# First expert's weights: one rounding instruction on ScalarE, remainders on VectorE instead of GpSimd

## The chip, the cores and the metric

The kernel runs on one core of a Trainium2 chip. A core has five engines with a queue of instructions each: TensorE (PE, with its weight loads PEld), VectorE (DVE), ScalarE (ACT), GpSimd (POOL) and SyncE (SP), which here issues most DMA transfers. The metric is the device time of one execution in microseconds, lower is better.

## What is computed

Attention with random features over 64 heads (8 batches of 8), then a mixture of experts in which each of 4608 tokens goes to one of eight experts.

```python
# attention, per batch and head; m = 128 features, D = 64
h = x_scaled @ omega.T - sum(x_scaled * x_scaled) / 2
phi = exp(h - max(h)) / sqrt(m)                 # for q and for k
kv = k_phi.T @ v;  z = sum(k_phi)
attn = (q_phi @ kv) / (q_phi @ z + 1e-6)
# experts, on x = attn as 4608 rows of 512
e = argmax(x @ w_gate);  gate = softmax(x @ w_gate)[e]
eom = sigmoid(x @ w_output_gate)
out = gate * eom[e] * (relu(x @ w1[e]) @ w2[e])  # w1: 512x1024, w2: 1024x512
```

## The kernel before

The 64 heads are taken in pairs of batches as 32 units of 1152 tokens (nine chunks of 128). The first eight units, u = 0 to 7, are handled in f32 by TensorE: a projection `pp` of three groups (L629, with GpSimd's squares L601 as one input), minima by VectorE (`mx`, L651) and biases (`nb`, L657), exponentials on ScalarE (`ex`, L670, tile `ef`), a sum over keys (`kv`, L766), a transposition of the queries (`tq`, L720), which ScalarE rounds to f16 (`th`, L725) and VectorE completes with the remainder (`tl`, L727), a product with the key sums (`pn`, L849) and a division on VectorE (`xf`, L858, L860, L862). GpSimd then splits the result into an f16 half and a remainder (`xs`, L880 and L884) and adds up gate logits (`lga`, L902). PSUM has eight banks; each of `pp`, `tq`, `kv` and `pn` takes one and holds it until the step that last reads it has run: `tl` for a `tq`, `ex` for a `pp`, the gate step `gl` (L816) for a `kv`, `xf` for a `pn`.

From unit 8 on the projection works with f16 halves and remainders. The first eight units make the first quarter of the tokens; then VectorE routes them (which expert, which place), writes a list, and GpSimd gathers the rows of the first items. An item is 128 tokens of one expert: two products with w1 and w2, each matrix kept as an f16 half (`w1h`, `w2h`) and an f16 remainder (`w1l`, `w2l`) so that three f16 products stand for one in f32.

The weights of the expert that is taken first (`FIRST = 1`) are loaded during the attention of the first units, in eight quarters of 128 x 1024: four of w1 and four of w2. SyncE loads a quarter into `r1` or `r2`; ScalarE multiplies it in place by 64 (step `w0s`, `scale_up`, L484); ScalarE rounds it to f16 (`w0h`, `rounded`, L488); GpSimd subtracts (`w0l`, `remainder`, L492). Weights of later experts are treated otherwise: `high` (L462) scales and rounds in one activation, `low` (L468) makes the remainder from the raw weights in one scalar_tensor_tensor on VectorE.

Nothing is scheduled at run time: a step is added to a plan with `plan.add` (its key, engine, what it comes after), and the table `ORDER` lists the steps by number in the order in which they are emitted. So each engine's queue is that table, cut to the engine. `BANKS` gives each step that needs a bank its number. An engine runs its queue in order and waits at an instruction until what it depends on is done.

Of the kernel before, what the change touches and what calls it, by code (L numbers as in the profile page):

```python
# [14 lines left out]
AF = mybir.ActivationFunctionType  # L15
# [312 lines left out]
def attention_moe(ctx: ExitStack, tc: tile.TileContext, kqt, kqn, v, om, wg, w1, w2, cf, cm, ci, out):  # L328
# [146 lines left out]
    def first_weights():  # L475
# [6 lines left out]
        def scale_up(which, i):  # L482
            src, _, _, sc = quarter(which, i)
            nc.scalar.activation(src, src, AF.Copy, scale=sc)  # L484

        def rounded(which, i):
            src, hi, _, _ = quarter(which, i)
            nc.scalar.copy(hi, src)  # L488
# [1385 lines left out]
```

## Time and profile before

| | us |
|---|---|
| median of three runs | 619.28 (617.71 to 622.87) |
| profiled execution, its time | 620.54 |
| profiled execution, its span | 618.5 |
| TensorE busy | 594.8 (96%) |
| TensorE weight loads | 471.3 (76%) |
| VectorE busy | 386.0 (62%) |
| ScalarE busy | 420.6 (68%) |
| GpSimd busy | 376.2 (61%) |

The shares are averages over the span. The stretches differ: the first eight units run to about 77 us, then come the units from 8 on together with the first routing, and from about 110 us the first items of the experts run beside the rest of the attention. Times in the rows below count from the start of the span.

### The profile page before, as it was taken

The page shows a single profiled execution, that of the slowest core. Times are in us where ns is not written, and L with a number is a line of the kernel's source. Part 1 is how long each engine was busy: PE and PEld are TensorE (multiplying, and loading weights), DVE is VectorE, ACT ScalarE, POOL GpSimd, SP SyncE. Part 2 cuts the span into 40 slices and gives each one's busy share as a digit, 9 for nine tenths or more (in the row PEclk, how much of TensorE's full clock was granted, in tenths as well). Part 3 has the DMA queues.
Part 4 walks back from the last instruction along what each step waited for, and adds up shares of the span by engine and source line. Part 5 has one row for each costly group of instructions (what it writes and reads, how often), then busy time and mean ns, then how long its engine had stood idle before and what let it go on. Part 6 is the DMA issues. An engine that isn't in the chain of part 4 may idle for free. (4 is left out here: it accounts for less than half of the span.)

```text
span 618.5 us, 22153 instructions
## 1 busy us (share of the span) xinstructions
PE 594.8 (96%) x8736; PEld 471.3 (76%) x8736; DVE 386.0 (62%) x1220; ACT 420.6 (68%) x978; POOL 376.2 (61%) x275
## 2 busy tenths in 40 slices
PE   8999987999999999999999999999999999999995
PEld 8999876877796777778777777778867587777775
DVE  4877699876678887657797856543693351162143
ACT  6999999779888688889958787872431341351244
POOL 2265689788977879997897889985322122121203
PEclk9999997899999999999999999999999899999999
DMA  8655688999999999989978999777586935942391
GB/s 282 196 158 159 212 274 212 233 236 257 305 251 217 254 281 242 269 188 238 304 199 251 247 192 203 171 170 222 193 176 189 245 82 109 300 117 69 104 278 50
DMA packets 146022, 128.86 MB, mean 208 GB/s; under 512 B 104286, under 2 KB 127584, under 8 KB 144608
## 3 DMA queue, kind: packets, MB, share of 16 engines
q1 hardware_dynamic: 139904, 107.45, 68.6%
q0 software_dynamic: 5984, 19.72, 10.1%
q8 instruction: 73, 1.20, 0.8%
q14 instruction: 61, 0.50, 0.3%
HBM read 83.86 MB, written 19.30 MB: 167 GB/s over the span
## 5 line engine op out<-in xcount | busy, mean ns | idle before, releaser
L1661 PE MATMUL ph<-xt,w1h 128*128 128x128 f16 (+1 forms) x2368 | 200.4, 218 | 2.2 <-ACT ef L670 0.7
L1661 PE MATMUL ph<-xt,w1l 128*128 128x128 f16 (+1 forms) x1184 | 196.6, 218 | 0.9 <-issue 0.9
L1661 PEld LDWEIGHTS <-w1h 128*128 128x128 f16 x2368 | 178.2, 98 | 9.6 <-issue 2.4
L670 ACT ACTIVATE ef<-pp,nb 128x128 f32<-128x128 f32 x576 | 163.7, 397 | 15.7 <-DVE nb L664 11.4
L651 DVE TENSOR_REDUCE pp<-pp 128x3 f32<-128x384 f32 x192 | 103.0, 557 | 35.2 <-PE pp L629 29.0
L693 POOL TENSOR_TENSOR es<-ef,es 128x1152 f16<-128x1152 f32 x44 | 104.8, 2390 | 25.8 <-ACT es L691 15.2
L1661 PEld LDWEIGHTS <-w1l 128*128 128x128 f16 x1184 | 115.2, 98 | 1.6 <-issue 1.6
L1672 DVE SCALAR_TENSOR_TENSOR hl<-ph,hh 128x512 f16<-128x512 f32 (+1 forms) x76 | 50.4, 664 | 95.2 <-ACTq L1555 53.5
L1693 PE MATMUL po<-w2h,hh 128*128 128x512 f16 x280 | 106.9, 382 | 0.4 <-ACT es L691 0.4
L1693 PE MATMUL po<-w2l,hh 128*128 128x512 f16 x280 | 106.8, 382 | 0.0
L1693 PE MATMUL po<-w2h,hl 128*128 128x512 f16 x280 | 106.7, 381 | 0.0
L1668 ACT ACTIVATE hh<-ph 128x512 f16<-128x512 f32 (+1 forms) x76 | 44.5, 591 | 85.5 <-PE ph L1661 65.7
L1693 PEld LDWEIGHTS <-hh 128*128 128x128 f16 x560 | 51.5, 98 | 53.7 <-issue 1.9
L1617 POOL DMA_INDIRECT gx<-rows,gi x38 | 39.5, 1038 | 83.3 <-ACT os L1772 34.4
L551 POOL TENSOR_TENSOR xlo<-xt,xhi 128x1152 f16<-128x1152 f32 x24 | 57.3, 2386 | 9.8 <-ACT xhi L544 8.0
L691 ACT CAST es<-ef 128x1152 f16<-128x1152 f32 x44 | 51.5, 1180 | 3.0 <-DMA et<-es 2.3
L1693 PEld LDWEIGHTS <-hl 128*128 128x128 f16 x280 | 27.5, 98 | 33.8 <-issue 0.8
L1772 ACT ACTIVATE os<-po,gx 128x512 f32<-128x512 f32 (+1 forms) x34 | 23.3, 686 | 43.5 <-PE po L1693 39.7
L849 PE MATMUL pn<-kvs,et 128*128 128x81 f16 (+1 forms) x960 | 47.9, 204 | 2.2 <-DVE nb L664 0.7
L849 PEld LDWEIGHTS <-et 128*128 128x128 f16 (+1 forms) x960 | 40.5, 101 | 9.3 <-issue 1.8
L629 PE MATMUL pp<-omh,xhi 64*128 64x128 f16 x432 | 42.9, 223 | 2.3 <-ACT ef L670 0.9
L1759 POOL DMA_INDIRECT out<-os,oi x25 | 26.6, 1065 | 27.7 <-ACT os L1772 22.9
(215 smaller groups left out, 1093.6 us busy)
## 6 DMA issues: line engine op xcount, KB each, us to landing
r<-w SPq DMA_DIRECT2D x10, 2048.0 KB
xt<-kqt SPq DMA_DIRECT2D x31, 576.0 KB
xn<-kqn SPq DMA_DIRECT2D x24, 576.0 KB
rawv<-v SPq DMA_DIRECT2D x32, 325.0 KB
rows<-xs SPq DMA_DIRECT2D x16, 576.0 KB
r<-w SPq DMA_DIRECT2D x8, 512.0 KB
ef<-w SPq DMA_DIRECT2D x2, 512.0 KB
et<-w SPq DMA_DIRECT2D x2, 512.0 KB
```

The costliest lines, as they stand in the source:

```text
L551: lambda t0=t0, t1=t1: nc.gpsimd.tensor_tensor(out=xl(u)[:, t0:t1], in0=xt32(u)[:, t0:t1], in1=xh(u)[:, t0:t1], op=ALU.subtract),
L629: nc.tensor.matmul(banks["pp", 2 * u + i, g][:, c, :], x[r, t], w[r, :], start=(a == 0), stop=(a == len(ops) - 1))
L651: nc.vector.tensor_reduce(out=pp[:, 3, 0:3], in_=pp[:, 0:3, :], op=ALU.min, axis=AX.X)
L670: nc.scalar.activation(ef(n)[:, c, :], banks["pp", n, g][:, c % 3, :], AF.Exp, bias=nb(n)[:, c : c + 1], scale=-SK)
L691: nc.scalar.copy(es(slot_es(n))[:, 0], ef(n))
L693: nc.gpsimd.tensor_tensor(out=es(slot_es(n))[:, 1], in0=ef(n), in1=es(slot_es(n))[:, 0], op=ALU.subtract)
L849: nc.tensor.matmul(pn[lo:hi, c - c0, :], a[:, c, lo:hi], w[:, :, b], start=(i == 0), stop=(i == len(ops) - 1))
L1617: nc.gpsimd.indirect_dma_start(out=gx(n), out_offset=None, in_=rows[0 : (j + 1) * NC * P], in_offset=bass.IndirectOffsetOnAxis(ap=tabs[gr] ...
L1661: nc.tensor.matmul(ph[:, f4, 0:w_], w[qd][:, kk, fo : fo + P], xt(n)[:, x, 0:w_], start=(a == 0), stop=(a == 3 * KC - 1))
L1668: nc.scalar.activation(hh(n)[:, sl, 0:w_], banks["ph", n, g][:, :, 0:w_], AF.Relu)
L1672: nc.vector.scalar_tensor_tensor(out=hl(n)[:, sl, 0:w_], in0=banks["ph", n, g][:, :, 0:w_], scalar=0.0, in1=hh(n)[:, sl, 0:w_], op0=ALU.ma ...
L1693: nc.tensor.matmul(po, x(n)[:, f, :], w[f // 2][:, f % 2, :], start=(f == 0 and a == 0), stop=(f == FC - 1 and a == 2))
```

## The change

The two ScalarE steps of a quarter, `w0s` and `w0h`, become one step `w0h` that calls `high`, the function of the later experts. The step `w0l` calls `low` on VectorE instead of `remainder` on GpSimd. The plan has 3310 steps instead of 3318, and all others stand in the same order; `BANKS` is unchanged.

```diff
-        def scale_up(which, i):
-            src, _, _, sc = quarter(which, i)
-            nc.scalar.activation(src, src, AF.Copy, scale=sc)
-
-        def rounded(which, i):
-            src, hi, _, _ = quarter(which, i)
-            nc.scalar.copy(hi, src)
-
-        def remainder(which, i):
-            src, hi, lo, _ = quarter(which, i)
-            nc.gpsimd.tensor_tensor(out=lo, in0=src, in1=hi, op=ALU.subtract)
-
...
                 plan.add(
-                    ("w0s", *key), ("ACT",), 0.95, lambda which=which, i=i: scale_up(which, i), after=[("w0", *key)], rank=R
+                    ("w0h", *key), ("ACT",), 0.95, lambda which=which, i=i: high(which, i), after=[("w0", *key)], rank=R
                 )
                 plan.add(
-                    ("w0h", *key), ("ACT",), 0.95, lambda which=which, i=i: rounded(which, i), after=[("w0s", *key)], rank=R
-                )
-                plan.add(
-                    ("w0l", *key), ("POOL",), 2.1, lambda which=which, i=i: remainder(which, i), after=[("w0h", *key)], rank=R
+                    ("w0l", *key), ("DVE",), 1.22, lambda which=which, i=i: low(which, i), after=[("w0h", *key)], rank=R
                 )
```

The functions that are now called for the first expert, too:

```python
def high(which, i, aside=False, n=None):
    src, hi, lo, sc = quarter(which, i, aside)
    ...
    nc.scalar.activation(hi, src, AF.Copy, scale=sc)

def low(which, i, aside=False, n=None):
    src, hi, lo, sc = quarter(which, i, aside)
    ...
    nc.vector.scalar_tensor_tensor(out=lo, in0=src, scalar=sc, in1=hi, op0=ALU.mult, op1=ALU.subtract)
```

The table `ORDER` is rewritten, since every number shifts; what it does is seen in the queues. From L492 on the line numbers of the changed kernel are 15 lower than before: L727 becomes L712, L651 L636, L657 L642, L816 L801, L788 L773, L862 L847.

VectorE's queue early in unit 0, before: the gate weights, the three `tl` steps of unit 0 (`et` from `tq`), then a minimum.

```order
L394 TENSOR_SCALAR wgs<-wgr 128x256
L395 SCALAR_TENSOR_TENSOR wgs<-wgr,wgs 128x256
L727 TENSOR_TENSOR et_283<-tq_1_260,et_283 128x384
L727 TENSOR_TENSOR et_283<-tq_0_250,et_283 128x384
L727 TENSOR_TENSOR et_283<-tq_2_269,et_283 128x384
L651 TENSOR_REDUCE pp_2_306<-pp_2_306 128x3
```

The same place of the changed kernel:

```order
L394 TENSOR_SCALAR wgs<-wgr 128x256
L395 SCALAR_TENSOR_TENSOR wgs<-wgr,wgs 128x256
L468 SCALAR_TENSOR_TENSOR w1l_95<-r_107,w1h_91 128x1024
L712 TENSOR_TENSOR et_283<-tq_1_260,et_283 128x384
L712 TENSOR_TENSOR et_283<-tq_0_250,et_283 128x384
L712 TENSOR_TENSOR et_283<-tq_2_269,et_283 128x384
L636 TENSOR_REDUCE pp_2_306<-pp_2_306 128x3
```

The remainder of w1's first quarter has come between the gate weights and the three `tl` steps.

VectorE's queue in unit 3, before: minima and biases, `tl` for groups 2 and 0 of unit 3 with unit 2's gate step between, and the key sums (`kvs`) of unit 3.

```order
L651 TENSOR_REDUCE pp_0_660<-pp_0_660 128x3
L651 TENSOR_REDUCE pp_1_691<-pp_1_691 128x3
L651 TENSOR_REDUCE pp_1_690<-pp_1_690 128x3
L657 TENSOR_SCALAR nb_718<-pp_1_690 128x3
L657 TENSOR_SCALAR nb_720<-pp_1_691 128x3
L727 TENSOR_TENSOR et_754<-tq_2_722,et_754 128x384
L816 SCALAR_TENSOR_TENSOR kvs_614<-kv_582,kvs_614 128x2x16
L727 TENSOR_TENSOR et_754<-tq_0_729,et_754 128x384
L788 SCALAR_TENSOR_TENSOR kvs_762<-kv_733,kvs_762 128x2x65
```

The same place of the changed kernel:

```order
L636 TENSOR_REDUCE pp_0_660<-pp_0_660 128x3
L468 SCALAR_TENSOR_TENSOR w2l_106<-r_108,w2h_102 128x1024
L636 TENSOR_REDUCE pp_1_691<-pp_1_691 128x3
L636 TENSOR_REDUCE pp_1_690<-pp_1_690 128x3
L642 TENSOR_SCALAR nb_719<-pp_1_690 128x3
L642 TENSOR_SCALAR nb_721<-pp_1_691 128x3
L712 TENSOR_TENSOR et_754<-tq_2_723,et_754 128x384
L801 SCALAR_TENSOR_TENSOR kvs_613<-kv_582,kvs_613 128x2x16
L468 SCALAR_TENSOR_TENSOR w1l_97<-r_107,w1h_93 128x1024
L712 TENSOR_TENSOR et_754<-tq_0_730,et_754 128x384
L773 SCALAR_TENSOR_TENSOR kvs_762<-kv_734,kvs_762 128x2x65
```

Two remainders are new here: w2's last quarter ahead of two minima, w1's third quarter between unit 2's gate step and the `tl` step that frees a bank of `tq`.

GpSimd's queue at its last remainders and the first gather, before (`es` and `xlo` are remainders of the attention, `gx` the gathered rows, `gi` the list that VectorE writes):

```order
L693 TENSOR_TENSOR es_1840<-ef_1775,es_1840 128x1152
L492 TENSOR_TENSOR w2l_104<-r_108,w2h_100 128x1024
L551 TENSOR_TENSOR xlo_1865<-xt_1755,xhi_1842 128x1152
L492 TENSOR_TENSOR w1l_96<-r_107,w1h_92 128x1024
L1555 UNCONDITIONAL_BRANCH x2
L1617 DMA gx_2315<-rows,gi_2092 128x528
```

The same place of the changed kernel:

```order
L678 TENSOR_TENSOR es_1836<-ef_1771,es_1836 128x1152
L536 TENSOR_TENSOR xlo_1858<-xt_1751,xhi_1838 128x1152
L1540 UNCONDITIONAL_BRANCH x2
L1602 DMA gx_2307<-rows,gi_2084 128x528
```

The two remainders are gone from GpSimd's queue ahead of the gather, and nothing has taken their place.

## Rows read from the trace of the kernel before

**Rows 1.** Table of stretches: bounds, length, busy time per engine, TensorE's granted clock, DMA.
```profile
core 0: us, PE busy (x) PEld busy (x) DVE busy (x) ACT busy (x) POOL busy (x), PEclk, DMA share, GB/s
8.00:73.00 65.00, 64.99 (x918) 60.83 (x916) 48.41 (x158) 61.35 (x184) 32.06 (x24) 1.00 0.62 197
77.00:110.00 33.00, 26.28 (x391) 23.07 (x391) 31.57 (x136) 30.45 (x89) 29.46 (x19) 0.84 0.84 233
125.00:480.00 355.00, 349.32 (x5458) 269.49 (x5456) 244.04 (x809) 263.98 (x599) 273.76 (x196) 1.00 0.92 229
```
**Rows 2.** TensorE's groups, 8 to 73 us: busy us, mean ns, idle time ahead.
```profile
L629 PE MATMUL pp<-omf,xt 64*128 64x128 f32 x260 | 27.8, 283 | 0.0
...
L810 PE MATMUL kv<-wgs,kvf 128*128 128x32 f16 x18 | 1.4, 177 | 0.0
```
**Rows 3.** Instructions on tile w1h: count, ns least/median/most, first and last start.
```profile
L462 ACT ACTIVATE w1h<-r x16: 1040/1047/1057, 174.3 to 547.4; 128x1024 f16<-128x1024 f32 x16
L468 DVE SCALAR_TENSOR_TENSOR w1l<-r,w1h x16: 1212/1218/1749, 175.6 to 548.6; 128x1024 f16<-128x1024 f32 x16
L488 ACT CAST w1h<-r x4: 1037/1072/1142, 23.3 to 64.6; 128x1024 f16<-128x1024 f32 x4
L492 POOL TENSOR_TENSOR w1l<-r,w1h x4: 2126/2134/2137, 68.9 to 107.1; 128x1024 f16<-128x1024 f32 x4
```
**Rows 4.** VectorE's timeline near 188 us: start, us, operation, count, idle before.
```profile
187.87 4.49 DVE L468 SCALAR_TENSOR_TENSOR w2l<-r,w2h 128x1024 f16<-128x1024 f32 x3 [1.24 <-ACT w2h L462]
```
**Rows 5.** GpSimd's timeline near 188 us.
```profile
187.55 1.44 POOL L714 TENSOR_TENSOR vs<-rawv,vs 128x650 f16<-128x650 f32 x1
```
**Rows 6.** VectorE's timeline near 102 us.
```profile
101.94 1.35 DVE L1065 TENSOR_TENSOR place<-cmt,rt 128x1152 f16<-128x1152 f16 x1
```
**Rows 7.** GpSimd's timeline near 102 us.
```profile
100.34 2.38 POOL L693 TENSOR_TENSOR es<-ef,es 128x1152 f16<-128x1152 f32 x1
```
**Rows 8.** Timelines of VectorE, GpSimd and TensorE, 14 to 19 us.
```profile
15.31 1.37 DVE L394 TENSOR_SCALAR wgs<-wgr 128x256 f16<-128x256 f32 x1
16.71 0.43 DVE L395 SCALAR_TENSOR_TENSOR wgs<-wgr,wgs 128x256 f16<-128x256 f32 x1
17.41 1.49 DVE L727 TENSOR_TENSOR et<-tq,et 128x384 f16<-128x384 f32 x3 [0.28 <-ACT et L725]
...
14.42 2.11 POOL L601 TENSOR_TENSOR xn<-xt 128x1152 f32<-128x1152 f32 x1 [4.27 <-DMA xt<-kqt]
...
18.51 0.36 PE L629 MATMUL pp<-half,xn 64*128 64x128 f32 x1
```
**Rows 9.** Timelines of VectorE and TensorE, 36 to 39 us.
```profile
36.55 0.57 DVE L651 TENSOR_REDUCE pp<-pp 128x3 f32<-128x384 f32 x1 [0.36 <-PE pp L629]
...
37.49 0.17 DVE L858 TENSOR_SCALAR den<-pn 128x5 f32<-128x5 f32 x1 [0.17 <-PE pn L849]
...
38.23 0.56 DVE L862 TENSOR_TENSOR xf<-pn,den 128x400 f32<-128x400 f32 x1
...
38.80 0.27 PE L629 MATMUL pp<-omf,xt 64*128 64x128 f32 x1
```
**Rows 10.** Timelines of VectorE, GpSimd, ScalarE and TensorE, 41 to 45 us.
```profile
42.40 0.55 DVE L727 TENSOR_TENSOR et<-tq,et 128x384 f16<-128x384 f32 x1
...
42.18 2.11 POOL L601 TENSOR_TENSOR xn<-xt 128x1152 f32<-128x1152 f32 x1 [0.60 <-DMA xt<-kqt]
...
41.91 1.08 ACT L484 ACTIVATE r<-r 128x1024 f32<-128x1024 f32 x1
...
44.77 0.49 PE L629 MATMUL pp<-omf,xt 64*128 64x128 f32 x4
```
**Rows 11.** Timelines of VectorE and TensorE, 48 to 50 us.
```profile
48.05 0.55 DVE L727 TENSOR_TENSOR et<-tq,et 128x384 f16<-128x384 f32 x1
...
49.23 0.95 PE L766 MATMUL kv<-rawv,ef 128*128 128x130 f32 x7
```
**Rows 12.** Timelines of VectorE and TensorE, 63 to 65 us.
```profile
63.58 0.55 DVE L727 TENSOR_TENSOR et<-tq,et 128x384 f16<-128x384 f32 x1
...
64.63 0.49 PE L629 MATMUL pp<-omf,xt 64*128 64x128 f32 x4
```

270 rows, old and new, of the table ORDER are left out of this document.

## The prediction

> **What bounds the kernel now.** I read the table of stretches first [rows 1]. From 8 to 73 us, where all eight quarters of the first expert's weights arrive and their rounding is done, TensorE is busy 64.99 of 65 us at full granted clock, ScalarE 61.35, VectorE 48.41, GpSimd 32.06. The list of TensorE's groups in that stretch [rows 2] says the same in another way: none of its seven groups (the first and the last are shown) had any idle time ahead of it. So TensorE bounds 8–73 us, and ScalarE, though 94% busy, is never waited for. From 77 to 110 us the order turns over: VectorE is busy 31.57 of 33 us, TensorE 26.28 and its granted clock is 0.84. This is the second attention stage together with the first routing, and VectorE bounds it. From 125 to 480 us TensorE is busy 349.32 of 355 us. Whatever delays TensorE before 73 us therefore has nowhere to be made up: it shifts the start of the VectorE stretch, and that shifts what comes after.
>
> **What is removed.** ScalarE loses eight rounding instructions of about 1.08 us (L488 in [rows 3]), 8.6 us in all; the scaling instruction becomes the rounding one (the same form exists as L462, 1.05 us) at the same place. Price: nothing, in either direction, because the stretch where ScalarE gets lighter is TensorE's (0.0 of waits in [rows 2]). GpSimd loses eight subtractions of 2.13 us (L492 in [rows 3]), 17.0 us. The last one starts at 107.1 us [rows 3], late in the stretch that VectorE bounds, and what follows it on GpSimd is the first gather, which needs a list that VectorE makes. Price: nothing again.
>
> **What is added.** VectorE gets eight subtractions of the form L468, 1.22 us each [rows 3]. Consecutive VectorE instructions overlap a little: three L727 take 1.49 us together [rows 8] and one takes 0.55 [rows 10], a pitch of 0.47, so 0.08 is hidden and each insertion costs its successors 1.14 us. That is 9.1 us of VectorE work in a stretch where VectorE is idle 16.6 of 65 us. So most of it could be absorbed; the question is at which of the eight places the next VectorE instruction gives TensorE a PSUM bank that it needs at once. I walked through them in program order.
>
> - First quarter of w1, straight behind the gate weights (L394, L395). L395 ends at 17.14 and the three L727 begin at 17.41, having waited for ScalarE [rows 8]. With the new instruction they begin at 17.06 + 1.14 = 18.20, later by 0.79. The second of them ended at 17.41 + 0.47 + 0.55 = 18.43 and gives back the bank in which TensorE's group at 18.51 starts [rows 8]. Slack there is almost nothing: TensorE **+0.77**.
> - First quarter of w2 and last quarter of w2 stand ahead of a reduction (L651) that waits for TensorE, and the third quarter of w2 ahead of an L727 that waits for ScalarE's casts. These holes hide them: **0**. Without the cover each would cost up to 1.14.
> - Second quarter of w1, ahead of the reduction at 36.55, which had waited 0.36 for TensorE. The new instruction starts behind the previous one at about 36.11 and ends 0.70 after the reduction could begin. The later idle of 0.17 and small gaps leave 0.43 at the division L862, which ends at 38.79; TensorE's group at 38.80 writes into the bank that it frees [rows 9]: **+0.43**.
> - Third quarter of w1, ahead of the L727 at 42.40. Its rounded half comes from ScalarE: the instruction at 41.91 ends at 42.99 [rows 10], with the 1.20 already lost 44.19. If it starts then, L727 ends about 45.9 and TensorE's group at 44.77 [rows 10], now due at 45.97, is just met: 0. But GpSimd's squares (L601, 2.11 us, before at 42.18) are pushed to about 43.95 by the work ahead of them (the neighbouring quarter's subtraction delays GpSimd's small sums). If VectorE must let them finish, it starts at 46.06, L727 runs 47.20–47.75, and TensorE waits from 45.97: **+1.8**.
> - Fourth quarter of w1, straight ahead of the L727 at 48.05, which ended at 48.60. With 1.14 more it ends at 49.74, against TensorE's group at 49.23 [rows 11], with some wake-up time: **+0.6**.
> - Second quarter of w2, straight ahead of the L727 at 63.58, end 64.13; with 1.14 more 65.27, against TensorE's group at 64.63 [rows 12]: **+0.65**.
>
> Must VectorE let GpSimd finish? In the trace a subtraction L468 that met GpSimd's L714 took longer: three of them cover 4.49 us where three pitches and an overlap would be 3.5, and GpSimd's L714 ran 187.55 to 188.99 across the first [rows 4, 5]. L394 of 256 columns took 1.37 us beside L601 (14.42 to 16.53) and ended just behind it, where L395, of the same 256 columns and with nothing beside it, took 0.43 [rows 8]. Against it: the 1152-column L1065 (1.35 us) ran inside GpSimd's L693 and was not stretched [rows 6, 7]. The first two are the nearest in form (an f32 source and L468 itself), so I take the +1.8, with the 0 as the other bound.
>
> The Trainium skill has a rule for this ("SBUF — State Buffer", section "SBUF: two separate sides"): a VectorE operation with two SBUF inputs and a GpSimd operation share a port pair that is an exclusive lock, and whichever starts first holds it for its whole instruction. The 4.49 us agree with it, the L1065 does not obviously. By the rule the third quarter of w1 costs the 1.8, without it 0: the sum would be 4.25 or 2.45.
>
> **Sum.** 0.77 + 0.43 + 1.8 + 0.6 + 0.65 = 4.25 us. The profiled execution took 620.54 us, so it would take 624.8; it was 1.26 above the median of three runs, 619.28, and on that median the forecast is **623.5 us**. A measurement of this kernel can tell about 1% (6.2 us) from no change, so this would be a change within 1%.
>
> **Rivals.** (a) No lock at the third quarter: 2.45, so 621.7 us. For it: the difference in start is only 0.2 us, and L1065. (b) All eight fit into VectorE's idle 16.6 us: 619.3 us. Against it: five places where the slack read from the rows is under 0.5 us. (c) TensorE's new waits lower its clock. In 77–110, where TensorE is idle a fifth of the time, the granted clock, a mean over its two levels of 1.2 and 2.4 GHz, is 0.84 against 1.00 [rows 1]; that is 0.16 × 33 = 5.3 us of lost clock for waits of about 2 us each. The 1.8 us wait is as long, so about half of that on top: 4.25 + 2.6 = 6.9, 626 us, up to 628 with more waits. (d) The other side: the kernel gets faster. If ScalarE's 8 × 0.95 = 7.6 us of relief (the pitch of its rounding) came through, the time would be 611.7 us. It decides from the point where TensorE waits for ScalarE in 8–73; the 0.0 of [rows 2] speak against it.
>
> **How the numbers follow.** Forecast (lock, +4.25) 0.36; (a) 0.27; (b) 0.12; (c) 0.19; (d) 0.06. The range of 617.5 to 628.0 us takes in the forecast, (a), (b) and (c), with some 1.5 us of scatter on either side as the three runs show, and leaves out (d) and what exceeds (c): about 0.14. Faster by over 1% (below 613.1) is (d), 0.06; slower by over 1% (above 625.5) is (c) and the upper edge of the forecast, 0.22; the rest is 0.72.
>
> **What would show it.** In the profile after: TensorE's waits of 0.4 to 1.8 us on VectorE's L727 and L862 (in their new line numbers) at about 18.5, 39, 46, 50 and 66 us; ScalarE lighter by 8 to 9 us and GpSimd by 17, VectorE heavier by 10; L468 at about 46 us ending behind GpSimd's squares; the stretch behind 77 us as long as before, only shifted. Wrong would be the forecast if TensorE still shows no waits in 8–73 (b), if its granted clock falls below 1.00 there (c), or if the stretch after 77 us is shorter, which nothing here predicts.

## The result, and the profile after

The changed kernel takes 625.79 us as the median of 22 runs (620.4 to 631.58), the kernel before, timed beside it, 620.54 (617.47 to 624.25). The ratio is 1.0069 with a 95% interval of 1.0047 to 1.0092: 4.3 us slower (2.9 to 5.7); the ratio leaves out the two longest runs of the changed kernel, which count as a slower state. A later comparison has the same (e12 below, 1.0062). The forecast was 4.25 us slower, a change within 1%. Its 623.5 us stood on a median of 619.28 us for the kernel before, which is 620.54 here: of the 2.3 us by which it missed the time, 1.3 lie there.

The profiled execution took 628.51 us, above that median; its span is 626.7 us. So the two profiles differ by 8 us where the medians differ by 5, and a part of what the traces show must be scatter between executions. The table of stretches of the changed kernel, with the columns of [rows 1]:

```profile
8.00:73.00 65.00, 62.58 (x856) 57.92 (x854) 53.87 (x155) 52.15 (x166) 27.29 (x20) 1.00 0.58 180
77.00:110.00 33.00, 23.55 (x387) 20.17 (x385) 29.68 (x124) 30.03 (x84) 22.05 (x16) 0.99 0.89 243
110.00:125.00 15.00, 13.06 (x190) 11.45 (x190) 12.15 (x56) 12.23 (x38) 7.54 (x5) 0.73 0.86 228
125.00:480.00 355.00, 349.68 (x5453) 270.66 (x5452) 248.80 (x824) 267.13 (x604) 274.39 (x195) 1.00 0.93 228
```

From 8 to 73 us TensorE is no longer full: 62.58 us of 65 against 64.99 in [rows 1], and 856 matmul records against 918. ScalarE and GpSimd became lighter there, VectorE heavier. From 125 us on the picture is the same as before.

TensorE's waits from 17 to 83 us, in the changed kernel (engine, line, released by; total us, times, longest):

```profile
PE pp L614 <- DVE et L712: 1.6, 2, 1.4
PE kv L751 <- DVE et L712: 0.6, 1, 0.6
PE pp L614 <- DVE xf L847: 0.3, 1, 0.3
PE pp L614 <- DVE nb L642: 0.2, 1, 0.2
```

In the kernel before nothing waited up to 73 us [rows 2]. The third line is not new: it stands at 80.0 us, and the kernel before has the same wait at 75.3 us:

```profile
PE pp L629 <- DVE xf L862: 0.3, 1, 0.3
```

All new waits are for VectorE, none for ScalarE or GpSimd. What the view lists as a wait is shorter than the delay that goes with it (0.20 us are listed at 69.37 us, where TensorE loses 0.68), so the table further down goes by the starts of the instructions.

The longest of them is the one at the third quarter of w1. VectorE's, GpSimd's and TensorE's timelines of the changed kernel there (start, us, operation, idle before):

```profile
44.73 2.70 DVE L468 SCALAR_TENSOR_TENSOR w1l<-r,w1h 128x1024 f16<-128x1024 f32 x1 [0.53 <-ACT w1h L462]
47.36 0.54 DVE L712 TENSOR_TENSOR et<-tq,et 128x384 f16<-128x384 f32 x1
...
44.25 2.10 POOL L586 TENSOR_TENSOR xn<-xt 128x1152 f32<-128x1152 f32 x1
...
47.96 0.49 PE L614 MATMUL pp<-omf,xt 64*128 64x128 f32 x4 [1.40 <-DVE et L712]
```

GpSimd's squares began 0.48 us before the remainder and ended at 46.35; the remainder ended 1.08 us later, as if it had begun only then. L712 came behind it, and TensorE waited 1.40 us for the bank. In [rows 10] the same step, there L727, stood in the queue without the remainder.

**Where the shift arises.** The n-th TensorE instruction is the same one in all these kernels, so its start in one trace less its start in the trace of before gives the shift of TensorE. The table has the growth of that shift over each place (the times are those of the trace of before), worked out for five kernels. The first two rows lie ahead of any remainder and have nothing to do with the places; what the first one is, the last section tells.

| place | forecast | changed | e12 (changed again) | e4 | e3 | e1 |
|---|---|---|---|---|---|---|
| up to 14 us (start) | 0 | 1.06 | 0.73 | 0.42 | 0.42 | 0.59 |
| 14–18.2, ahead of the first place | 0 | −0.14 | −0.14 | −0.62 | −0.62 | −0.21 |
| 18.2–18.8, w1 first quarter | 0.77 | 0.19 | 0.33 | 0.72 | 0.25 | 0.00 |
| 29.3–32.2, w2 first quarter | 0 | 0.13 | 0.12 | 0.13 | 0.13 | −0.01 |
| 38.1–39.4, w1 second quarter | 0.43 | 0.47 | 0.47 | 0.46 | 0.00 | 0.00 |
| 43.7–46.4, w1 third quarter | 1.8 | 1.47 | 1.47 | 0.00 | 0.00 | 0.00 |
| 46.4–50.8, w1 fourth quarter | 0.6 | 0.87 | 0.87 | 0.86 | 0.00 | 0.00 |
| 64.5–67.8, w2 second quarter | 0.65 | 0.68 | 0.68 | 0.68 | 0.00 | 0.00 |
| sum of the quarters | 4.25 | 3.81 | 3.94 | 2.85 | 0.38 | −0.01 |

From 83 us on it is scatter: the shift of the changed kernel's profiled execution is 4.74 us at 83 us and 8.34 at the end, that of e12, the same program, 4.54 and −3.34.

### The profile page after: what moved, and what is told of

Same layout as the page of the kernel before. It is cut to its first block, busy times and chain, and to the rows that moved or that the text cites. A ratio compares the mean times of both kernels' runs of the same rounds, so it can differ in the third digit from the quotient of the medians.

```text
span 626.7 us, 22148 instructions
## 1 busy us (share of the span) xinstructions
PE 596.2 (95%) x8736; PEld 473.0 (75%) x8736; DVE 395.9 (63%) x1228; ACT 416.1 (66%) x970; POOL 362.1 (58%) x267
## 5 line engine op out<-in xcount | busy, mean ns | idle before, releaser
L636 DVE TENSOR_REDUCE pp<-pp 128x3 f32<-128x384 f32 x192 | 102.9, 557 | 36.3 <-PE pp L614 31.2
L1757 ACT ACTIVATE os<-po,gx 128x512 f32<-128x512 f32 (+1 forms) x34 | 23.4, 687 | 43.2 <-PE po L1678 39.4
```

Source lines behind the costliest of these rows:

```text
L636: nc.vector.tensor_reduce(out=pp[:, 3, 0:3], in_=pp[:, 0:3, :], op=ALU.min, axis=AX.X)
```

## The experiments

**What is the price of VectorE's remainders alone?** In e1 they are left out, with the rest of the change kept.

```diff
+        for i in range(NQ):
+            nc.vector.memset(w1l[i], 0.0)
+            nc.gpsimd.memset(w2l[i], 0.0)
...
-                    ("w0l", *key), ("DVE",), 1.22, lambda which=which, i=i: low(which, i), after=[("w0h", *key)], rank=R
+                    ("w0l", *key), ("DVE",), 1.22, lambda which=which, i=i: None, after=[("w0h", *key)], rank=R
```

> The changed kernel with the eight VectorE remainders of the first expert left out (the f16 remainders are zeros, written once at the start), so it has the lighter ScalarE and the lighter GpSimd and nothing on VectorE. Theory (VectorE's insertions alone cost, the relief of ScalarE and GpSimd is worth nothing because TensorE never waits for them in 8-73 us): the time of the kernel before, within 1 us, and no wait of TensorE on L712-type steps. Rival (the relief is worth something that the insertions eat up again): faster than before by 2 to 7.6 us.

Measured: ratio 1.0003 (0.9969 to 1.0036). TensorE's only wait from 17 to 83 us, and the stretch 8–73 in the columns of [rows 1]:

```profile
PE pp L617 <- DVE xf L850: 0.3, 1, 0.3
...
8.00:73.00 65.00, 65.00 (x913) 61.04 (x912) 47.80 (x157) 55.34 (x177) 25.44 (x21) 1.00 0.63 199
```

ScalarE is 6 us and GpSimd 6.6 us lighter in that stretch than before, TensorE is full in both, and the time is the same within 0.4%: the relief gives nothing by itself that can be seen, and the loss comes with VectorE's remainders.

**And ScalarE's part alone?** e2 is the kernel before with one rounding instruction per quarter.

```diff
         def scale_up(which, i):
-            src, _, _, sc = quarter(which, i)
-            nc.scalar.activation(src, src, AF.Copy, scale=sc)
+            src, hi, _, sc = quarter(which, i)
+            nc.scalar.activation(hi, src, AF.Copy, scale=sc)
 
         def rounded(which, i):
-            src, hi, _, _ = quarter(which, i)
-            nc.scalar.copy(hi, src)
+            pass
```

> The kernel before with ScalarE's part of the change alone: scaling and rounding in one instruction at the place of the old scaling, nothing at the place of the old rounding; GpSimd still makes the remainders, at its old places (it subtracts from the unscaled weights, the scaling of that operand is left out). Theory: the time of the kernel before within 1 us (619.5 to 621.5). Rival (ScalarE, 94% busy in 8-73 us, is what VectorE and through it TensorE waits for): faster by up to 7.6 us.

Measured: ratio 1.0015 (0.9982 to 1.0048). In the stretch 8–73 us ScalarE has 55.89 us instead of 61.35, TensorE 65.00:

```profile
8.00:73.00 65.00, 65.00 (x922) 60.92 (x919) 48.32 (x157) 55.89 (x178) 32.33 (x24) 1.00 0.62 199
```

The rival of a gain of up to 7.6 us is excluded: the interval's lower end is a gain of 1.1 us.

**Is it the work or the place?** e3 moves five remainders in the table of the order, nothing else.

```diff
 # VectorE's queue, by steps
-w0l(w1,0) ahead of tl(0,1)
+w0l(w1,0) ahead of kvs(4)
-w0l(w1,1) ahead of mx(7,2)
+w0l(w1,1) ahead of kvs(2)
-w0l(w1,2) ahead of tl(3,0)
+w0l(w1,2) ahead of mx(14,0)
-w0l(w1,3) ahead of tl(4,1)
+w0l(w1,3) ahead of xf(5,0), first step
-w0l(w2,1) ahead of tl(5,1)
+w0l(w2,1) ahead of mx(15,2)
```

> The changed kernel with the five remainders that were costed at more than nothing moved in VectorE's queue to places where VectorE was idle for 0.6 to 1.5 us in the trace of before (w1's quarters ahead of the key sums of unit 4, the key sums of unit 2, a minimum of unit 7 and the division of unit 5; w2's second quarter ahead of a minimum of unit 7). Theory (the place decides): within 1 us of the kernel before; TensorE's waits on L712 and L847 in 8-77 us gone, 4 us less than in the changed kernel. Rival (VectorE's 9.1 us more work costs wherever it stands, or the clock does): slower than before by about 4 us, as the changed kernel.

Measured: ratio 0.9986 (0.9959 to 1.0013), 0.83% or 5.1 us under the changed kernel's ratio. From 17 to 83 us TensorE's only wait is that of e1 and of the kernel before:

```profile
PE pp L613 <- DVE xf L846: 0.3, 1, 0.3
```

VectorE does all its 9.1 us more, and by the interval they cost 0.8 us at most: the place decides. Nor does this version beat the kernel before by anything that can be told from no change. There is nothing to be gained, since what got lighter was not waited for.

**Do VectorE and GpSimd exclude each other at the third quarter?** e4 keeps the squares behind the remainder.

```diff
+                    if u == 5:
+                        nc.gpsimd.tensor_copy(seen, w1l[2][:, 0, 0:1])
                     nc.gpsimd.tensor_tensor(out=y, in0=x, in1=x, op=ALU.mult)
...
 # table of the order: the squares of unit 5 are moved behind w0l of w1's third quarter
```

> The changed kernel with GpSimd's squares of unit 5 kept behind the remainder of w1's third quarter by a copy of one column of that remainder (nothing left out). Theory (VectorE and GpSimd exclude each other for that pair of instructions): the remainder takes 1.22 us instead of 2.70, TensorE's wait of 1.40 us at 47.96 us is gone or below 0.3, the shift of TensorE at 60 us against the kernel before is 1.4 us less than in the changed kernel. Rival (the instruction was long for another reason, or TensorE waits for ScalarE's late half anyway): 2.7 us and the wait stay.

Measured: ratio 1.0049 (1.0021 to 1.0076). VectorE and GpSimd in e4:

```profile
44.13 1.23 DVE L468 SCALAR_TENSOR_TENSOR w1l<-r,w1h 128x1024 f16<-128x1024 f32 x1 [0.53 <-ACT w1h L462]
...
45.42 0.19 POOL L587 COPY seen<-w1l 128x1 f16<-128x1 f16 x1 [1.74 <-DVE w1l L468]
45.56 2.11 POOL L588 TENSOR_TENSOR xn<-xt 128x1152 f32<-128x1152 f32 x1
```

The remainder stands at the same place, waits the same 0.53 us for ScalarE and takes 1.23 us instead of 2.70. TensorE's shift over the place is 0.00 instead of 1.47 (table above), and the terms behind it stay. So the 1.47 us is the price of meeting the squares, and the insertion alone would have been hidden there. In the times the two kernels differ by 0.2% of uncertain size; the traces decide this one.

**Which instructions are shut out?** Five kernels change that one instruction. Each ran once, so only its trace counts.

```diff
-            low(which, i)                                   # w1's third quarter alone
+ e6          nc.vector.tensor_tensor(out=lo, in0=hi, in1=hi, op=ALU.subtract)
+ e7          nc.vector.tensor_scalar(lo, src, sc, None, ALU.mult)
+ e8          nc.vector.tensor_scalar(hi, src, sc, None, ALU.mult)
+ e9          nc.vector.tensor_scalar(lo, hi, 0.0, None, ALU.mult)
+ e10         nc.vector.tensor_tensor(out=lo, in0=hi, in1=hi[:, :, 0:1].broadcast_to([P, KC, FQ]), op=ALU.subtract)
```

> The changed kernel with one instruction changed: the remainder of w1's third quarter subtracts the f16 half from itself (a tensor_tensor with two f16 inputs in SBUF; the remainder of that quarter is left out, it becomes zero). It meets GpSimd's squares at 44-46 us as before. If every VectorE instruction with two SBUF inputs is shut out while GpSimd works, it ends behind the squares, 2.5 to 2.7 us after its start. If what matters is the f32 source (as L1065 of the kernel before, two f16 inputs, suggests), it takes 1.2 us or less and TensorE's wait of 1.40 us is gone.

> The changed kernel with one instruction changed: in place of the remainder of w1's third quarter a tensor_scalar with one input (the f32 weights times 64 rounded to f16; the subtraction of that quarter is left out). If two SBUF inputs are what is shut out, it takes 1.2 us or less beside GpSimd's squares and TensorE's wait of 1.40 us is gone. If an f32 input alone is enough, as the 1.37 us of L394 beside the squares of unit 2 suggest, it ends behind the squares and the wait stays.

> The changed kernel with one instruction changed: in place of the remainder of w1's third quarter a tensor_scalar with one f32 input that writes the rounded half a second time, so that it must wait for ScalarE's rounding and meets GpSimd's squares (the remainder of that quarter is left out, it stays zero). e7 showed 0.72 us for such an instruction that had started ahead of the squares. If two SBUF inputs are what is shut out, 0.7 us here too, and TensorE waits less than 0.3 us at 45-48 us. If the one-input form is shut out as well, as L394 suggests, it ends 0.7 us behind the squares, 2.0 to 2.4 us after its start, and TensorE waits about 0.9 us.

> As e8 with an f16 input (the rounded half times zero; the remainder of that quarter is left out). If one input goes beside GpSimd whatever its type: at most 0.7 us. If the fast form of an instruction is what needs GpSimd's path: it ends behind the squares, about 2 us after its start.

> As e6 with a repeated second operand: a tensor_tensor of two f16 inputs, the second one column per row repeated along the row, as in L1065 of the kernel before (the remainder of that quarter is left out). e6, without the repeated operand, took 2.15 us and ended 0.54 us behind the squares. If the repeated operand is why L1065 ran inside GpSimd's work: about 1.2 us, not stretched. If not: again behind the squares, 2.1 to 2.8 us.

The instruction and the squares that it met, VectorE ahead of GpSimd, first of e6, then of e7, e8, e9 and e10:

```profile
44.49 2.15 DVE L486 TENSOR_TENSOR w1l<-w1h 128x1024 f16<-128x1024 f16 x1 [0.53 <-ACT w1h L462]
...
43.99 2.11 POOL L592 TENSOR_TENSOR xn<-xt 128x1152 f32<-128x1152 f32 x1
```

```profile
43.83 0.72 DVE L486 TENSOR_SCALAR w1l<-r 128x1024 f16<-128x1024 f32 x1
...
44.26 2.26 POOL L592 TENSOR_TENSOR xn<-xt 128x1152 f32<-128x1152 f32 x1 [0.25 <-DMA xt<-kqt]
```

```profile
44.13 2.28 DVE L487 TENSOR_SCALAR w1h<-r 128x1024 f16<-128x1024 f32 x1 [0.53 <-ACT w1h L463]
...
43.76 2.11 POOL L593 TENSOR_TENSOR xn<-xt 128x1152 f32<-128x1152 f32 x1
```

```profile
44.12 1.90 DVE L486 TENSOR_SCALAR w1l<-w1h 128x1024 f16<-128x1024 f16 x1 [0.53 <-ACT w1h L462]
...
43.63 2.11 POOL L592 TENSOR_TENSOR xn<-xt 128x1152 f32<-128x1152 f32 x1
```

```profile
44.09 2.69 DVE L486 TENSOR_TENSOR w1l<-w1h 128x1024 f16<-128x1024 f16 x1 [0.53 <-ACT w1h L462]
...
43.60 2.10 POOL L592 TENSOR_TENSOR xn<-xt 128x1152 f32<-128x1152 f32 x1
```

e7 missed its aim: the instruction does not read the rounded half, so it did not wait for ScalarE, began 0.43 us ahead of the squares and took 0.72 us; it gives the undisturbed time of that form. In the others the squares came first and ended at 46.10, 45.87, 45.74 and 45.70; VectorE's instruction ended 0.54, 0.54, 0.28 and 1.08 us later. So all of them were shut out: two inputs or one, f16 or f32. (What the forms of e6, e9 and e10 take undisturbed no run shows.) TensorE's shift over the place follows: 0.92, 1.05, 0.67 and 1.46 us in these four, 0.00 in e7. The expectations that one input goes through and that two f16 inputs do fell with that, and so did the one that the repeated operand is what let L1065 run beside GpSimd's work [rows 6, 7].

The kernel has another difference that bears on L1065: its second operand `rank` is cut from `banks["rt", j]`, so it lies in PSUM (all of `banks` are tiles of the PSUM pool), while every operand of L468 and of e6 to e10 lies in SBUF. No run changes this alone, but rows of the kernel before agree. L727 reads `tq` from PSUM; it took 0.55 us at 42.40, wholly inside GpSimd's squares [rows 10], and 0.55 at 63.58 [rows 12], where GpSimd did nothing. L1065 itself took 1.35 us at 101.94, beside L693 for its first 0.78 us (not inside it throughout, as the prediction has it) and then beside L492, and the same 1.35 at 461.61 with no GpSimd tensor_tensor beside it:

```profile
102.67 2.13 POOL L492 TENSOR_TENSOR w2l<-r,w2h 128x1024 f16<-128x1024 f32 x1
...
461.61 1.35 DVE L1065 TENSOR_TENSOR place<-cmt,rt 128x1152 f16<-128x1152 f16 x1
```

**Does ScalarE's relief matter once the remainders stand on VectorE?** e5 puts ScalarE's second instruction back, straight behind the first; e11 does so for six quarters, without the first of w1 and of w2.

```diff
+        def two_steps(which, i):
+            src, hi, _, sc = quarter(which, i)
+            if i == 0:                                                # e11 alone
+                nc.scalar.activation(hi, src, AF.Copy, scale=sc)
+                return
+            nc.scalar.activation(src, src, AF.Copy, scale=sc)
+            nc.scalar.copy(hi, src)
```

> The changed kernel with ScalarE's part undone: the first expert's quarters are scaled in place and then rounded by a second instruction right behind, so ScalarE has its 8.6 us back; VectorE's remainders stand where the change put them. Theory (ScalarE's relief is worth nothing): slower than the kernel before by 4 to 5 us, as the changed kernel (ratio 1.006 to 1.009), with the same waits of TensorE on VectorE at 47, 53 and 69 us. Rival (the change gained on ScalarE what it lost elsewhere): slower than the changed kernel by 2 to 7 us, ratio above 1.010.

Measured: ratio 1.0118 (1.0077 to 1.0160), above the changed kernel's 1.0069 (1.0047 to 1.0092) by its middle, though the intervals overlap. Its trace has a wait for ScalarE that no other kernel had up to 83 us: TensorE at 16.62 us, behind the four ScalarE instructions that now stand ahead of unit 0's exponentials:

```profile
16.62 0.84 PE L714 MATMUL tq<-ident,ef 128*128 128x128 f32 x3 [1.55 <-ACT ef L664]
...
10.59 1.06 ACT L484 ACTIVATE r<-r 128x1024 f32<-128x1024 f32 x1
11.68 1.04 ACT L485 CAST w1h<-r 128x1024 f16<-128x1024 f32 x1
...
13.39 1.06 ACT L484 ACTIVATE r<-r 128x1024 f32<-128x1024 f32 x1
14.49 1.04 ACT L485 CAST w2h<-r 128x1024 f16<-128x1024 f32 x1
```

> As e5, but ScalarE's second instruction is put back for six quarters alone; the first quarter of w1 and of w2, which stand ahead of unit 0's exponentials, keep the one instruction of the change. e5's trace shows TensorE waiting 1.6 us for ScalarE's exponentials at 16 us, behind four such instructions. Theory (that place is most of what made e5 slower than the changed kernel): no such wait, the shift of TensorE at 83 us against the kernel before is 4.2 to 5.2 us less what the start differs, ratio 1.006 to 1.009. Rival (ScalarE's 8.6 us cost about 3 us spread over all places): ratio 1.010 to 1.012 again, with new waits for ScalarE after 40 us.

> The changed kernel again, beside e11 on the same chip: ratio 1.005 to 1.009 as it was. TensorE's start-up in the first 10 us differs from execution to execution; if TensorE is not late there, the first quarter of w1 costs 0.7 us at 18.5 us instead of 0.2, and the shift of TensorE between 17 and 83 us is 4.3 us.

Measured, beside each other: e11 1.0141 (1.0092 to 1.0190), e12 1.0062 (1.0027 to 1.0096). e12 is as it was; TensorE was late again in its first 14 us (0.73), so the 0.7 us expected for the first quarter of w1 in the other case could not be seen (0.33). e11 is not as the changed kernel: the wait for ScalarE at 16 us is gone, as expected, but the time did not come down, and by its interval e11 stays above the 1.006 to 1.009 of the theory. The rival had the ratio nearly right, but the waits of TensorE for ScalarE after 40 us that it expected are not there. The trace shows a small part of the reason. At the third quarter VectorE waits three times as long for ScalarE's half:

```profile
15.31 2.03 DVE L394 TENSOR_SCALAR wgs<-wgr 128x256 f16<-128x256 f32 x1
...
17.72 1.22 DVE L492 SCALAR_TENSOR_TENSOR w1l<-r,w1h 128x1024 f16<-128x1024 f32 x1
...
46.06 1.63 DVE L492 SCALAR_TENSOR_TENSOR w1l<-r,w1h 128x1024 f16<-128x1024 f32 x1 [1.61 <-ACT w1h L488]
...
15.09 2.11 POOL L598 TENSOR_TENSOR xn<-xt 128x1152 f32<-128x1152 f32 x1 [4.83 <-ACT ef L667]
```

That changes nothing there, since the squares would have held it up anyway (shift 1.48). But the second quarter of w2 costs 1.11 us instead of 0.68. The first of w1 costs 1.43, because L394 met the squares of unit 2 early and was held 2.03 us; that is not the work of ScalarE's second instruction, since up to there e11 has the queues of the changed kernel. In the trace of e11 the shift grows by 5.4 us between 17 and 83 us, in that of e5 by 5.8 us from 14 us on, against 3.8 and 3.9 (from 17 us) of the changed kernel. So in the traces ScalarE's second instruction costs 0.4 us in e11, apart from the first quarter, and 2.0 us in e5, of which the wait at 16 us is the most. The times have 0.5 and 0.8% (3 and 5 us) over the changed kernel, with intervals nearly as wide. What lies beyond the traces' 2.0 and 0.4 us is not explained; the profiled execution of e11 was the fastest of its six (618.72 us, median 622.81).

## Why the prediction was right, point by point

- **TensorE bounds 8–73 us and its shift passes through.** Right. The sum of the terms in the traces is 3.81 and 3.94 us, the times give 4.3 (2.9 to 5.7) and 3.8 (1.7 to 5.9, from e12's ratio). So by the times nothing to speak of was made up behind 77 us. That 4.25 came so close is in part luck: the single terms missed by −0.58, 0.13, 0.04, −0.33, 0.27 and 0.03 us in the changed kernel's trace, which add up to −0.44, and the times leave 2.9 to 5.7 us open.
- **Removed work is worth nothing.** Right for the kernel before: e1 and e2 have it at 1.0003 and 1.0015. It needs a limit: in e5's trace a second ScalarE instruction, straight behind the first, costs 2.0 us once the remainders stand on VectorE. The merging of ScalarE's two steps brought no time, but at the new places an earlier half is worth something.
- **w1 first quarter, 0.77.** Too much in the changed kernel's two traces (0.19, 0.33). The 0.72 of e4 does not bear it out: e3 has no remainder at this place and the same shifts ahead of it (0.42, −0.62), and it shows 0.25, so the remainder is worth 0.47 there. The step took the time of L394, ahead of the remainder, as fixed, though the prediction itself reads it as held up by GpSimd's squares of unit 2. It took 1.37 us before [rows 8] and 0.80 after, because VectorE came to it 0.91 us later and the squares began only 0.34 later:

```profile
16.22 0.80 DVE L394 TENSOR_SCALAR wgs<-wgr 128x256 f16<-128x256 f32 x1
...
17.39 1.22 DVE L468 SCALAR_TENSOR_TENSOR w1l<-r,w1h 128x1024 f16<-128x1024 f32 x1
...
14.76 2.11 POOL L586 TENSOR_TENSOR xn<-xt 128x1152 f32<-128x1152 f32 x1 [4.61 <-DMA xt<-kqt]
```

  In e5 L394 came behind the squares, at 17.40, and took 0.28 us; there the term is 0.00, since the wait for ScalarE stands ahead of it. So this term depends on the execution, from 0.0 to 1.43 us over the kernels with a remainder here.
- **w2's three hidden quarters, 0.** Nearly: the first of w2 costs 0.13 in every kernel that has it, the other two nothing.
- **w1 second quarter, 0.43; w2 second quarter, 0.65.** Right in size: 0.47 and 0.68. At the second quarter of w1 the profile puts the wait (0.22 us at 40.65) down to the biases L642, one step behind the division L847 that the forecast named; the division had ended at 40.50.
- **w1 third quarter, 1.8 against 0.** The mechanism was right and shown by e4: 2.70 us against 1.23. The size was 1.47; the wait was reckoned from squares starting at 43.95 with a shift of 1.20, and they started at 44.25 with a shift of 1.71, so 0.2 us earlier in the course of the program. The argument against the mechanism, L1065, falls away if an operand in PSUM is what lets it through (above).
- **w1 fourth quarter, 0.6.** 0.87. VectorE was later there than the forecast had it. Before, a reduction ahead of it in VectorE's queue had waited 0.27 us for TensorE, at 46.43; in the changed kernel it began at 49.83 without a wait, which less TensorE's shift of 3.18 is 46.65. That is 0.2 us later by TensorE's count, as if so much of the third quarter's insertion had not been absorbed yet; e4 has the same 0.86.
- **Rival (c), the clock.** It did not come. In the changed kernel's trace the records of the granted clock have the higher level from 10.26 to 109.25 us, through all the new waits. The spells at 1.2 GHz moved from 77–110 us to 110–125 (0.84 to 0.99, and 0.89 to 0.73), and they are no longer than before: by the records 13.7 us before (96.25–103.08 and 106.49–113.32) and 10.3 after (109.25–116.08 and 122.90–126.32). The row of before for the second stretch is

```profile
110.00:125.00 15.00, 14.09 (x212) 12.72 (x212) 12.41 (x52) 11.13 (x29) 12.18 (x8) 0.89 0.99 240
```

- **The signs to look for.** Of the five waits forecast four are in the list; the one at 18.5 us is too short for it. ScalarE's line of the page was to be 8 to 9 us lighter and GpSimd's 17; they are 4.5 and 14.1, VectorE's 9.9 heavier:

```profile
PE 596.2 (95%) x8736; PEld 473.0 (75%) x8736; DVE 395.9 (63%) x1228; ACT 416.1 (66%) x970; POOL 362.1 (58%) x267
```

  GpSimd's instructions are held up by VectorE's remainders in turn. Its 17.0 us of subtractions are gone, but its casts `xs` took 1.9 us more in all and its copies `lga` 1.0, for instance a cast of 0.66 us that took 1.59 from just behind a remainder's start:

```profile
51.44 1.22 DVE L468 SCALAR_TENSOR_TENSOR w1l<-r,w1h 128x1024 f16<-128x1024 f32 x1
...
51.59 1.59 POOL L865 CAST xs<-xf 128x576 f16<-128x576 f32 x1 [5.24 <-DVE xf L847]
```

  ScalarE's instructions went as forecast: L484 and L488 had 8.8 and 8.6 us, the eight L462 in their place have 8.6. The page counts time once in which two records of an engine overlap; summed one by one, ScalarE's records fell by 12.5 us and their overlap by 8.0, which leaves the 4.5.

## What to carry to other kernels

Taking work from engines that nobody waits for gives nothing, however busy they are; putting work on another engine is priced at the places where it is put, one by one, by the next instruction there that frees something the bounding engine needs. The same 9.1 us of VectorE work cost 4 us at the changed kernel's places and 0.8 us at most in holes of 0.6 to 1.5 us (e3). When an instruction on VectorE that works in SBUF alone stands near one of GpSimd, look at which of them starts first: 0.5 us of head start cost 1.5 us here.

## What the runs showed of the hardware

GpSimd's tensor_tensor held up every form of VectorE instruction that was put beside it at w1's third quarter, all with their operands in SBUF: the scalar_tensor_tensor with an f32 and an f16 input (2.70 us instead of 1.22), a tensor_tensor of two f16 inputs (2.15, and 2.69 with a repeated operand), and also tensor_scalar with one f32 or one f16 input (2.28 against 0.72 undisturbed in e7, and 1.90). The Trainium skill ("SBUF — State Buffer", section "SBUF: two separate sides") names VectorE operations with two SBUF inputs and those in a two-port mode as the ones that contend with GpSimd; the five traces agree with that if the one-input forms, 0.72 us for 1024 columns in e7, are taken as such a mode, which no run here shows by itself. Not held up were L727 and L1065 of the kernel before, each with an operand in PSUM (above), and L562, a reduction with one f32 input in SBUF: it took 1.34 us inside GpSimd's L551 as at 206.95 us, where no GpSimd tensor_tensor was beside it.

```profile
153.18 1.34 DVE L562 TENSOR_REDUCE sqs<-sqt 128x18 f32<-128x1152 f32 x1
...
152.54 2.39 POOL L551 TENSOR_TENSOR xlo<-xt,xhi 128x1152 f16<-128x1152 f32 x1
...
206.95 1.34 DVE L562 TENSOR_REDUCE sqs<-sqt 128x18 f32<-128x1152 f32 x1
```

TensorE's first matmuls are issued at about half the rate for a time that differs between executions of the same instructions. From 9 to 10 us the kernel before and the changed kernel show

```profile
9.00:10.00 1.00, 1.00 (x22) 1.00 1.01 392
```

```profile
9.00:10.00 1.00, 1.00 (x12) 1.00 1.03 405
```

22 and 12 matmuls. The clock column has 1.00 in both, but that is no record: the trace's records of the granted clock begin at 7.50 us in the kernel before, at 10.26 in the changed kernel and at 9.58 in e12, each with the higher level, and ahead of the first one the view has nothing to take off. In all three traces the rate goes up at that time, so the slow start is put down here to the lower level of the clock (1.2 against 2.4 GHz), by the rate alone. That is where the changed kernel's trace lost its first 1.06 us, ahead of any instruction that the change had touched; the other kernels lie between −0.1 and 0.7 there. What makes the clock rise later in one execution than in another stays open. A comparison of single traces has to take that off first.
